# The low halves of the converted weights are subtracted on GpSimd in place of VectorE

## The chip, the cores and the metric

The kernel runs on one core of a Trainium2 chip. The metric is the device time of one execution, in microseconds (us). The kernel before was timed three times: 1189.03, 1189.84 and 1190.34 us, so the median is 1189.84 us. A core has five engines with instruction queues of their own: TensorE (PE, with the loading of its weights shown apart as PEld), VectorE (DVE), ScalarE (ACT), GpSimd (POOL) and SyncE (SP), which here issues all DMAs. Each queue is worked through in order; between queues there are semaphores.

## The reference

A linear attention is followed by a two-layer network. With batch 8, 8 heads, sequence 576 and head size 64:

```
proj = x @ w_phi;  proj -= max|proj| over the features
phi(x) = concat(exp(proj), exp(-proj))          # 2 x 128 features
kv = phi(k)^T v,   z = sum phi(k)
attn = (phi(q) kv) / (phi(q) z + 1e-6)
x = attn as 4608 tokens x 512
h = x @ w_in (512 x 2048);  g = max(0.01 h, h);  out = g @ w_out (2048 x 512)
```

The weights w_in and w_out arrive as 64-bit floating-point numbers, everything else as 32-bit ones. The result is in 32 bits.

## The kernel before

**Split products.** Most matrix products run in the type fp32r, which keeps fewer bits than fp32. To lose little, an operand a is split into a high half, a cast to fp32r, and a low half, a minus the high half, and a product becomes three: high by high, high by low and low by high. The high half is a cast (`copy_`, line 64), the low half a subtraction (`tt_`, line 71). Both helpers ask `pick` (line 59), which looks up an engine in the table `ENG` (line 35) by a key and goes round its letters: "v" is VectorE, "a" ScalarE, "p" GpSimd. A key that is not in the table gets ScalarE for a cast and GpSimd for a two-operand operation. So the low halves xl (of the attention's output), gl (of the first layer's result), ql and most of kpl (of the features) and vl run on GpSimd; the key "l", which belongs to the weights, says "v".

**The conversion of the weights.** `load_weights` (lines 161 to 187) takes w_in and w_out in 16 slices each, 32 steps in turn: w_in slice 0, w_out slice 0, w_in slice 1 and so on. A step loads 128 x 512 numbers of 64 bits (512 KB, line 172) into a staging place: halves of the ring in the first 10 steps, then parts of early buffers (f4, f1), then qs and the ring again. It builds the 32-bit numbers from the two words of each: the absolute value of the upper word (ScalarE, line 177) goes into w, a tile with the tag ql, clamped (VectorE, 178), shifted and masked (179) and joined with the two top bits (180); the lower word is scaled into cr, tag kvl (ScalarE, 182), and added (183, both as 32-bit whole numbers). Then come the high half (ScalarE, line 185, shown as line 67) and the low half (line 186, shown as line 72). The results stay in SBUF: the tiles w0h, w0l, w1h and w1l, each of 4 slices. The tag ql has two buffers, so step n+2 begins to write when the low half of step n has been read; kvl has one.

**The layers.** The tokens are worked through in 18 blocks of 256. `layer1` (line 592 on) is 12 matmuls of 128 x 256 for one slice: at each of four depths w0h and w0l with xh (lines 595 and 596), then four of w0h with xl (598). Leaky ReLU follows on ScalarE (602), then gh and gl. `layer2` adds to an accumulator in PSUM: w1h with gh (615), w1l with gh (616), w1h with gl (617). It runs three steps behind `layer1`. The first two blocks go through the 16 slices in alternation, so that each slice is used twice once it is converted; the others follow one by one with all slices in SBUF.

**The attention.** `k_phase` and `q_phase` work on pairs of heads. The first batch has its own functions (`first_k_phase`, `first_q_phase`), run before and beside the first conversion steps. In `first_q_phase` each pair goes through projection (425), maximum and subtraction (VectorE, 507 and 509), transposition on TensorE (515), exponentials (ScalarE, 522 and 523), product (537), copies to the ring and dn (ScalarE, 540 and 541), reciprocals of the denominators through two transpositions (VectorE, 544 to 547), and a multiplication into the ring on GpSimd. `split` makes xh (ScalarE) and xl (GpSimd) of it. In later batches, lines 216, 296 and 347 are low halves written out on VectorE. `load_k` and `load_q` load the next pair; after the v loads, a memset on GpSimd (198) fills two columns of the tile rv.

**The order.** It is not written out by hand. Each instruction has a priority, set by `tc.cur_priority`: the first batch comes ahead of the rest of the attention, that ahead of the conversion (`PW`), and this ahead of the layers. A scheduler simulates the engines and puts on each the ready instruction of the highest priority; the order of each queue is fixed then, and the chip follows it.

Of the kernel before, what the change touches and what calls it, by code (L numbers as in the profile page):

```python
# [31 lines left out]
NK = 8  # L32
BUFS = {"kk": 4, "pmk": 2, "eq": 2, "m4": 3, "m4n": 2, "g": 2, "gh": 2, "gl": 2, "qh": 2, "ql": 2, "dn": 2}
PBUFS = {"a": 3, "c": 1, "h": 2, "acc": 2}
ENG = {"vh": "a", "kst": "v", "qh": "v", "o": "av", "kpl": "pppv", "ksub": "vvp", "l": "v"}
TINY = 2.0 ** -15
HUGE = 2.0 ** 16 * 1.875
PF = -10 ** 6
# [6 lines left out]
def attention_moe_kernel(ctx: ExitStack, tc: tile.TileContext, q, k, v, vt, w_phi, w_in, w_out, out):  # L45
# [13 lines left out]
    def pick(key):  # L59
        n = cnt[key] = cnt.get(key, -1) + 1  # L60
        e = ENG.get(key, "")
        return e[n % len(e)] if e else None
# [648 lines left out]
```

## Time and profile before

One execution was recorded by the profiler. Its own time is 1187.94 us, and its span, from the first instruction to the last, is 1186.2 us.

| | before |
|---|---|
| median of three runs | 1189.84 us |
| the profiled execution, its time | 1187.94 us |
| its span | 1186.2 us |
| granted TensorE clock | 1.00 |
| GpSimd subtractions for gl, number and mean | 288, 827 ns |
| conversion steps, number | 32 |
| first and last start of line 177 | 20.0 and 175.8 us |
| last low half of the weights starts | 184.5 us |

To read it: a group of the profile names the line, the engine, the operation, output and inputs, the shape, how often it ran, the busy time in us and the mean time of one in ns; behind the second bar stands the engine's idle time ahead of these instructions, and what ended it. The line is often that of a helper (67, 69 and 72 are the casts and two-operand operations of `copy_` and `tt_`), so the output's name tells which it is. Slices are fortieths of the span, 29.7 us each, in tenths of busy time. A wait is given as "who <- for whom: us in total, times, longest". TensorE's matmuls overlap each other, so a TensorE that is always busy may still have gaps of less than one matmul.

### The profile page before, as it was taken

The page shows a single profiled execution, that of the slowest core. Times are in us where ns is not written, and L with a number is a line of the kernel's source. Part 1 is how long each engine was busy: PE and PEld are TensorE (multiplying, and loading weights), DVE is VectorE, ACT ScalarE, POOL GpSimd, SP SyncE. Part 2 cuts the span into 40 slices and gives each one's busy share as a digit, 9 for nine tenths or more (in the row PEclk, how much of TensorE's full clock was granted, in tenths as well). Part 3 has the DMA queues.
Part 4 walks back from the last instruction along what each step waited for, and adds up shares of the span by engine and source line. Part 5 has one row for each costly group of instructions (what it writes and reads, how often), then busy time and mean ns, then how long its engine had stood idle before and what let it go on. Part 6 is the DMA issues. An engine that isn't in the chain of part 4 may idle for free.

```text
span 1186.2 us, 21604 instructions
## 1 busy us (share of the span) xinstructions
PE 1153.7 (97%) x7496; PEld 1026.5 (87%) x7496; DVE 769.2 (65%) x1326; ACT 861.3 (73%) x2266; POOL 632.7 (53%) x709
## 2 busy tenths in 40 slices
PE   8899999899998999999999999999999999999998
PEld 5677778799887989889999999999999989899997
DVE  5988995587788778777777777757777765200000
ACT  5978775878788778777888878868887785433232
POOL 0131222576576667666666666757666666433232
PEclk9999999999999999999999999999999999999999
DMA  8436331211111111111111111101111100000000
GB/s 218 135 91 168 103 108 36 70 41 34 51 33 50 34 34 29 42 34 30 52 33 51 33 51 26 48 23 40 33 50 34 40 3 20 1 19 9 10 19 18
DMA packets 71005, 57.88 MB, mean 49 GB/s; under 512 B 53232, under 2 KB 54512, under 8 KB 70896
## 3 DMA queue, kind: packets, MB, share of 16 engines
q1 hardware_dynamic: 70896, 56.51, 17.1%
q8 instruction: 59, 0.97, 0.3%
q14 instruction: 50, 0.41, 0.1%
HBM read 46.27 MB, written 9.44 MB: 47 GB/s over the span
## 4 chain that ended last, share of the span: by engine, by line
PE 47%; DVE 2%; DMA 1%; issue 0%; ACT 0%; POOL 0%; SPq 0%; DVEq 0%; ACTq 0%; POOLq 0%
PE h L598 6%; PE h L596 6%; PE h L595 6%; PE acc L616 6%; PE acc L617 6%; PE acc L615 6%; PE c L228 3%; PE a L409 1%; PE a L404 1%; PE a L406 1%; PE a L251 1%; PE a L365 1%; PE a L364 1%; DVE tq L381 0%; DMA mx<-mx 0%
## 5 line engine op out<-in xcount | busy, mean ns | idle before, releaser
L72 POOL TENSOR_TENSOR gl<-g,gh 128x256 fp32r<-128x256 f32 x288 | 237.3, 827 | 305.4 <-ACT gh L67 220.2
L595 PE MATMUL h<-xh,w0h 128*128 128x256 f32 x1088 | 278.8, 283 | 2.4 <-ACT xh L67 1.3
L596 PE MATMUL h<-xh,w0l 128*128 128x256 f32 x1088 | 276.6, 281 | 0.0
L595 PEld LDWEIGHTS h<-xh,w0h 128*128 128x128 f32 x1088 | 205.4, 189 | 12.4 <-ACT g L602 2.4
L615 PE MATMUL acc<-w1h,gh 128*128 128x512 f32 x544 | 214.3, 394 | 0.2 <-DVE o L69 0.2
L616 PE MATMUL acc<-w1l,gh 128*128 128x512 f32 x544 | 213.3, 392 | 0.0
L596 PEld LDWEIGHTS h<-xh,w0l 128*128 128x128 f32 x1088 | 205.3, 189 | 8.4 <-issue 0.4
L617 PE MATMUL acc<-w1h,gl 128*128 128x512 f32 x544 | 203.5, 395 | 2.6 <-POOL rv L198 1.2
L598 PE MATMUL h<-xl,w0h 128*128 128x256 f32 x1088 | 191.2, 281 | 0.0
L602 ACT ACTIVATE g<-h 128x256 f32<-128x256 f32 x288 | 108.3, 381 | 106.0 <-PE h L598 83.0
L72 POOL TENSOR_TENSOR ql<-eq,qh 128x576 fp32r<-128x576 f32 x96 | 142.9, 1500 | 53.3 <-DVE qh L395 44.3
L67 ACT CAST gh<-g 128x256 fp32r<-128x256 f32 x288 | 115.2, 403 | 63.0 <-PE acc L616 60.9
L598 PEld LDWEIGHTS h<-xl,w0h 128*128 128x128 f32 x1088 | 155.9, 188 | 0.9 <-issue 0.4
L72 POOL TENSOR_TENSOR kpl<-ek,kph 128x512 fp32r<-128x512 f32 x72 | 101.5, 1410 | 75.9 <-ACT kph L67 59.3
L617 PEld LDWEIGHTS acc<-w1h,gl 128*128 128x128 f32 x544 | 99.5, 188 | 19.5 <-POOL rv L198 1.4
L69 DVE COPY o<-acc 128x512 f32<-128x512 f32 x17 | 11.7, 688 | 161.0 <-DMA out_dram<-o 118.0
L615 PEld LDWEIGHTS acc<-w1h,gh 128*128 128x128 f32 x544 | 102.5, 188 | 12.1 <-DVE o L69 0.4
L616 PEld LDWEIGHTS acc<-w1l,gh 128*128 128x128 f32 x544 | 102.3, 188 | 11.7
L282 ACT ACTIVATE ek<-pmk,m 128x128 f32<-128x128 f32 (+1 forms) x240 | 89.5, 390 | 13.5 <-DVE m L259 13.1
L281 ACT ACTIVATE ek<-pmk,m4n 128x128 f32<-128x128 f32 (+1 forms) x240 | 90.1, 392 | 8.6 <-DVE m4n L265 3.9
L395 DVE TENSOR_REDUCE qh<-eq 128x576 fp32r<-128x576 f32 x96 | 69.0, 751 | 25.7 <-ACT eq L389 22.9
L256 DVE TENSOR_TENSOR pmk<-a,pmk 128x256 f32<-128x256 f32 (+1 forms) x120 | 49.6, 420 | 54.0 <-ACT pmk L67 52.0
(183 smaller groups left out, 2404.8 us busy)
## 6 DMA issues: line engine op xcount, KB each, us to landing
out_dram<-o SPq DMA_DIRECT2D x36, 256.0 KB, 2.1
rq<-in_q_dram SPq DMA_DIRECT2D x28, 288.0 KB, 2.9
rk<-in_k_dram SPq DMA_DIRECT2D x27, 288.0 KB, 2.8
rv<-in_v_dram SPq DMA_DIRECT2D x29, 256.0 KB, 3.5
ring<-in_w_in_dram SPq DMA_DIRECT2D x9, 512.0 KB, 3.7
f<-in_w_out_dram SPq DMA_DIRECT2D x7, 512.0 KB, 3.6
f<-in_w_in_dram SPq DMA_DIRECT2D x7, 512.0 KB, 3.6
ring<-in_w_out_dram SPq DMA_DIRECT2D x5, 512.0 KB, 3.8
```

The costliest lines, as they stand in the source:

```text
L67: nc.scalar.copy(o, i)
L72: (nc.vector if pick(key) == "v" else nc.gpsimd).tensor_tensor(o, a, b, op=op)
L281: nc.scalar.activation(ek[r, j, 0:F], pmk[r, h], AF.Exp, bias=m4n[r, h : h + 1])
L282: nc.scalar.activation(ek[r, j, F:256], pmk[r, h], AF.Exp, scale=-1.0, bias=m4[r, h : h + 1])
L395: nc.vector.tensor_reduce(qh, eq.unsqueeze(3), axis=AX.X, op=ALU.max)
L595: nc.tensor.matmul(ph, lhsT=weight(0, "h", ft)[:, d * P : d * P + P], rhs=xh[d], start=d == 0, stop=False)
L596: nc.tensor.matmul(ph, lhsT=weight(0, "l", ft)[:, d * P : d * P + P], rhs=xh[d], start=False, stop=False)
L598: nc.tensor.matmul(ph, lhsT=weight(0, "h", ft)[:, d * P : d * P + P], rhs=xl[d], start=False, stop=d == NP - 1)
L602: nc.scalar.activation(g, ph, AF.Prelu, alpha=0.01)
L615: nc.tensor.matmul(a, lhsT=gh[:, ts], rhs=weight(1, "h", ft), start=ft == 0, stop=False)
L616: nc.tensor.matmul(a, lhsT=gh[:, ts], rhs=weight(1, "l", ft), start=False, stop=False)
L617: nc.tensor.matmul(a, lhsT=gl[:, ts], rhs=weight(1, "h", ft), start=False, stop=ft == NFT - 1)
```

## The change

In the table of engines the key "l" says "p". `tt_("l", ...)` in line 186 is its only use, so all 32 subtractions of the conversion are issued on GpSimd. Operation, shape and operands stay the same; the semaphores and the order of all queues are made anew by the scheduler.

```diff
-ENG = {"vh": "a", "kst": "v", "qh": "v", "o": "av", "kpl": "pppv", "ksub": "vvp", "l": "v"}
+ENG = {"vh": "a", "kst": "v", "qh": "v", "o": "av", "kpl": "pppv", "ksub": "vvp", "l": "p"}
```

## The prediction

> **What bounds the kernel now.** I read the page first: engine shares, the slices, the chain.
>
> ```profile
> span 1186.2 us, 21604 instructions
> PE 1153.7 (97%) x7496; PEld 1026.5 (87%) x7496; DVE 769.2 (65%) x1326; ACT 861.3 (73%) x2266; POOL 632.7 (53%) x709
> ...
> PE   8899999899998999999999999999999999999998
> DVE  5988995587788778777777777757777765200000
> ACT  5978775878788778777888878868887785433232
> POOL 0131222576576667666666666757666666433232
> ...
> PE 47%; DVE 2%; DMA 1%; issue 0%; ACT 0%; POOL 0%; SPq 0%; DVEq 0%; ACTq 0%; POOLq 0%
> ```
>
> TensorE is busy nearly everywhere, and nearly all of the chain that could be followed back is TensorE's (47% of the span against 2% for VectorE). So time is only won or lost where TensorE stands idle. VectorE is fullest in slices 1 to 5 (30 to 180 us), where the weights are converted, and GpSimd is nearly empty there. Next, the busy time by stage: the stage in which the first conversion steps share the engines with the first attention phases (20 to 70), a pause, the rest of the conversion (85 to 186), and what follows.
>
> ```profile
> core 0: us, PE busy (x) PEld busy (x) DVE busy (x) ACT busy (x) POOL busy (x), PEclk, DMA share, GB/s
> 20.00:70.00 50.00, 43.19 (x214) 30.83 (x213) 46.37 (x93) 46.44 (x103) 9.87 (x12) 1.00 0.47 138
> 70.00:85.00 15.00, 14.85 (x86) 12.14 (x87) 10.71 (x26) 9.24 (x25) 4.72 (x7) 1.00 0.38 121
> 85.00:186.00 101.00, 98.86 (x540) 76.60 (x538) 92.61 (x165) 78.67 (x184) 21.85 (x29) 1.00 0.42 117
> 186.00:240.00 54.00, 50.07 (x312) 42.45 (x311) 28.82 (x53) 38.81 (x107) 23.71 (x33) 1.00 0.18 52
> 240.00:800.00 560.00, 551.71 (x3772) 505.73 (x3772) 420.48 (x705) 456.92 (x1236) 374.32 (x386) 1.00 0.14 38
> 800.00:1186.00 386.00, 379.18 (x2518) 347.16 (x2516) 161.46 (x271) 223.85 (x603) 197.03 (x230) 1.00 0.08 23
> ```
>
> TensorE's idle time is 50 - 43.19 = 6.81 us in 20:70, 101 - 98.86 = 2.14 us in 85:186, 3.93 us in 186:240, and 8.29 + 6.82 = 15.1 us in everything after 240. The stage from 20 to 70 is the only one in which the conversion could cost TensorE much: VectorE and ScalarE are both full there, with 3.63 and 3.56 us idle in 50. In 85:186 VectorE has 8.4 us idle of 101, but TensorE hardly waits.
>
> Last, I asked how early the low halves are ready. Here is the first and the last low half of w_in (16 there are, and 16 of w_out), each with its own first matmul: line 596 runs four matmuls a step, so the first of its 1152 uses w_in's slice 0, and the 121st slice 15.
>
> ```profile
> 25.26 0.69 DVE L72 TENSOR_TENSOR w0l<-ql,w0h 128x512 fp32r<-128x512 f32 x1
> ...
> 58.63 0.28 PE L596 MATMUL h<-xh,w0l 128*128 128x256 f32 x1
> ...
> 180.28 1.22 DVE L72 TENSOR_TENSOR w0l<-ql,w0h 128x512 fp32r<-128x512 f32 x1
> ...
> 212.75 0.28 PE L596 MATMUL h<-xh,w0l 128*128 128x256 f32 x1
> ```
>
> The first is done at 25.95 and used at 58.63, the last at 181.50 and used at 212.75: 32.7 and 31.3 us of margin. Counting the same way through all 32, no margin is under 31 us. The conversion is work done in advance; nobody on TensorE waits for a low half.
>
> **The change, part by part.** What leaves VectorE and what GpSimd takes over:
>
> ```profile
> L72 DVE TENSOR_TENSOR w0l<-ql,w0h 128x512 fp32r<-128x512 f32 x16 | 12.3, 766 | 0.1
> L72 DVE TENSOR_TENSOR w1l<-ql,w1h 128x512 fp32r<-128x512 f32 x16 | 11.5, 716 | 0.4
> L183 DVE CUSTOM_DVE_ANT_0 ql<-ql,kvl 128x1024 uint16<-128x1024 uint16 x32 | 22.2, 694 | 0.6
> L72 POOL TENSOR_TENSOR kpl<-ek,kph 128x512 fp32r<-128x512 f32 x72 | 101.5, 1410 | 75.9 <-ACT kph L67 59.3 <-PE acc L616 5.7 <-PE c L228 3.5
> ```
>
> Removed from VectorE: 12.3 + 11.5 = 23.8 us in 32 instructions. Added to GpSimd: the trace has the same operation and shape there, kpl, at a mean of 1410 ns, so 32 x 1.41 = 45.1 us. Its busy time from 20 to 186 us rises from 36 (9.87 + 4.72 + 21.85) to about 81 of 166 us, so GpSimd does not become the bound. That kpl runs on GpSimd in this very form also says that the change will do what it says. No DMA moves.
>
> The margin first: a low half is done later by 1.41 - 0.74 = 0.67 us plus a wait in GpSimd's queue. Against 31 us of margin that costs nothing; the cover is the 31 us themselves, and it would take a queue 20 instructions deep to use it up. In 85:186 the price is therefore near zero from this side, and the 22 instructions that VectorE loses there (16 us) gain near zero too, since TensorE has only 2.14 us to win.
>
> What counts is 20:70. What leaves VectorE there:
>
> ```profile
> 20.00:70.00 50.00, 1.36 (x5) 0.94 (x5) 3.91 (x5) 1.00 0.47 138
> ...
> 20.00:70.00 50.00, 0.78 (x2) 0.38 (x2) 3.05 (x4) 1.00 0.47 138
> ```
>
> (the third pair of busy time and count is VectorE's; first w_in's low halves, then w_out's): 3.91 + 3.05 = 6.96 us, nine instructions. But VectorE does not get all of it, because the two engines get in each other's way:
>
> ```profile
> 92.32 0.73 POOL L72 TENSOR_TENSOR gl<-g,gh 128x256 fp32r<-128x256 f32 x1 [0.20 <-ACT gh L67]
> ...
> 92.44 1.15 DVE L183 CUSTOM_DVE_ANT_0 ql<-ql,kvl 128x1024 uint16<-128x1024 uint16 x1
> ...
> L72 DVE TENSOR_TENSOR kpl<-ek,kph x24: 644/792/1593, 233.2 to 984.8; 128x512 fp32r<-128x512 f32 x24
> L296 DVE TENSOR_TENSOR kst<-ek,kst x24: 686/1186/1808, 238.4 to 987.1; 64x512 fp32r<-64x512 f32 x24
> ```
>
> A conversion instruction of line 183 (694 ns in the mean) started 0.12 us into a GpSimd subtraction and took 1.15 us, ending 0.54 us after it. The last two rows are VectorE instructions that often meet the long GpSimd subtractions (minimum/median/maximum ns): they reach 1593 and 1808 from minima of 644 and 686, with medians 0.15 and 0.50 us above the minimum. So a GpSimd low half costs VectorE somewhere between nothing and its own 1.3 us; I take the 0.50 of line 296, whose neighbours in time are just such subtractions. For nine: 4.5 us. VectorE's net relief in 20:70 is 6.96 - 4.5 = 2.5 us.
>
> Who profits from it? The waits in that stage:
>
> ```profile
> PE c L537 <- ACT eq L522: 1.9, 1, 1.9
> PE h L595 <- ACT xh L67: 1.3, 2, 0.7
> PE h L537 <- ACT dn L541: 1.0, 1, 1.0
> ...
> ACT ql L177 <- DVE w1l L72: 0.5, 1, 0.5
> ...
> PE a L515 <- DVE pm L509: 0.4, 1, 0.4
> ```
>
> TensorE's larger waits end on ScalarE (1.9, 1.3, 1.0 us), only a 0.4 us one on VectorE. ScalarE itself has 3.56 us idle to give, and what is late next when VectorE is faster is ScalarE, whose work stays the same. I credit half of the relief: -1.25 us.
>
> The added wait. A low half now waits in GpSimd's queue for the cast of the high half on ScalarE, and behind it stand the products with the reciprocal denominators (ring), the low halves of x (xl) and of g (gl), and the memset of the next v tile (rv), on which SP's queue waits:
>
> ```profile
> ACT g L602 <- POOL gl L72: 19.4, 28, 2.3
> PE acc L617 <- POOL gl L72: 0.8, 2, 0.6
> SPq L195 <- POOL rv L198: 12.4, 5, 4.0
> ```
>
> Over the whole run ScalarE waited 19.4 us for gl and TensorE 0.8, so GpSimd's queue seldom reaches TensorE. SP's 12.4 us of waits delay loads that are issued a head ahead of their use; at nothing, and if that cover were gone, one subtraction, 1.4 us, a load. In 20:70 a product delayed by one subtraction delays xh on ScalarE, for which TensorE waits already (1.3 us above): I add 1.0 us, between 0 and 2 x 1.41.
>
> The turn of the two buffers of ql. Line 177 of step n+2 writes the buffer that the low half of step n has read, and it stands in ScalarE's queue ahead of the exponentials. A turn that is tight today gets 0.67 us longer. In 20:70 the one such wait is 0.5 us: +0.7 us, between 0 and 8 x 0.67 = 5.4 us were all eight turns tight.
>
> Sum: -1.25 + 1.0 + 0.7 = +0.45 us. The profiled execution took 1187.94 us, 1.74 us more than its span, and 1.90 us less than the median of the runs; so 1188.4 for it and 1190.3 as a median. From no change a measurement here can tell about 0.2%, 2.4 us, so this is within it.
>
> **The rivals.** *The planner deals another order.* The scheduler places every instruction by simulated times, so 32 changed costs can move instructions long after the conversion. What it can win there is bounded by TensorE's idle 15.1 us after 240; a quarter of it, 3.8 us, in either direction gives 1186.0 or 1193.6. Against it: nothing after 186 us is edited. I give it 0.22, more of it upward (0.14) since the chain shows little left to win.
>
> *Slower: the shared access to SBUF decides, in 20:70.* If every low half on GpSimd holds VectorE up for as long as it runs, nine cost 9 x 1.3 = 11.7 us and save 6.96: VectorE needs 4.7 us more in a stage where it has 3.63 us idle, little of it usable since most is waiting for ScalarE. TensorE then comes later by up to 4.7 us: 1195.0. It decides from a price of 6.96/9 = 0.77 us a low half upward. For it: the 1.15 us above, and the maxima of 1593 and 1808. Against it: the medians, 0.15 and 0.50 us, lie under the threshold. [...] Chance 0.22.
>
> *Faster: VectorE's relief passes through.* If VectorE is what holds up ScalarE in 20:70 (it feeds the exponentials and the denominators), TensorE can win up to ScalarE's idle 3.56 us there, and a part of the 2.14 us in 85:186, say half: -4.6 us, 1185.2. For it: VectorE is the fullest of the helpers over 85:186 (92%). Against it: the waits above. Chance 0.16.
>
> **How the numbers follow.** My forecast, no change that can be told, has 0.40; its own range is 1187.5 to 1192.2. Slower is 0.22 + 0.14 = 0.36, faster 0.16 + 0.08 = 0.24. The range takes in 1185.2 and 1195.0, and beyond them the uncertain ends: the ql turns and the products at their upper bounds (5.4 and 2.8 us instead of 0.7 and 1.0) reach 1196.8, and the planner adds to either; 1184.5 to 1198.0, with about one in ten left out on each side.
>
> **What would show it.** Right: 32 new GpSimd rows of w0l and w1l at 1.3 to 1.45 us; VectorE's busy time in 20:186 lower by some 8 to 16 us rather than 24, with lines 178 to 183 longer in the mean; first uses of the low halves still over 25 us after them; TensorE's idle time in 20:70 within 2 us of 6.81. Wrong: TensorE waiting for w0l or w1l; TensorE's idle time in 20:70 over 10 or under 4 us; or a difference in the idle time after 240, which would be the planner's doing.

## The result and the profile after

| | before | after |
|---|---|---|
| median (lowest to highest), four runs each | 1189.43 us (1188.57 to 1190.34) | 1196.23 us (1195.41 to 1196.75) |
| profiled execution, its time | 1187.94 us | 1195.41 us |
| its span | 1186.2 us | 1193.6 us |
| granted TensorE clock | 1.00 | 0.995 |

The time after is 1.0059 times that before, with a 95% interval of 1.0044 to 1.0074: slower by 0.6%, 6.8 us between the medians. The page after, with its slices for VectorE and GpSimd:

```profile
span 1193.6 us, 21587 instructions
PE 1157.9 (97%) x7496; PEld 1031.1 (86%) x7496; DVE 762.9 (64%) x1294; ACT 863.2 (72%) x2266; POOL 672.8 (56%) x741
...
DVE  5978996567678678777777777767777776200000
...
POOL 0354553556676676656766676766666666433232
```

The 32 instructions have moved: VectorE's count is 1294 after 1326, GpSimd's 741 after 709, and GpSimd is no longer empty in slices 1 to 6. GpSimd's busy time rose by 40.1 us. VectorE's fell by 6.3 us only, where 23.8 us of subtractions left it. Next, the stages after (PE, PEld, DVE, ACT, POOL, then the clock):

```profile
20.00:70.00 50.00, 42.72 (x208) 31.00 (x207) 45.35 (x83) 45.32 (x100) 20.27 (x19) 0.97 0.48 136
70.00:85.00 15.00, 14.75 (x82) 11.76 (x80) 10.07 (x23) 8.97 (x25) 7.00 (x9) 1.00 0.31 90
85.00:186.00 101.00, 93.60 (x493) 71.02 (x492) 93.11 (x141) 77.41 (x176) 48.59 (x46) 0.98 0.42 120
186.00:240.00 54.00, 51.40 (x309) 43.30 (x307) 28.46 (x50) 36.60 (x99) 24.62 (x35) 1.00 0.15 37
240.00:800.00 560.00, 552.72 (x3785) 508.30 (x3785) 413.94 (x711) 459.13 (x1241) 372.45 (x387) 1.00 0.15 40
```

TensorE's idle time, stage length minus busy time, is where the loss shows. In 20:70 it is 7.28 us, 0.47 more than before. In 85:186 it is 7.40 us against 2.14: 5.3 us more. In 186:240 it is 2.60 against 3.93, and in 240:800 7.28 against 8.29, so part is given back. VectorE did 165 instructions in 85:186 before and 141 now, yet was busy for 93.11 us against 92.61. The work that left was made up for by the rest becoming longer. Here are the conversion's own VectorE lines, after and then before, as groups of instructions:

```profile
L183 DVE CUSTOM_DVE_ANT_0 ql<-ql,kvl 128x1024 uint16<-128x1024 uint16 x32 | 27.6, 861 | 4.3 <-ACT kvl L182 2.4
L179 DVE TENSOR_SCALAR ql<-ql 128x512 int32<-128x512 int32 x32 | 21.0, 658 | 0.5
L178 DVE TENSOR_SCALAR ql<-ql 128x512 f32<-128x512 f32 x32 | 17.2, 541 | 4.3 <-ACT ql L177 4.1
L180 DVE SCALAR_TENSOR_TENSOR ql<-f,ql 128x512 int32<-128x512 int32 x14 | 14.3, 1025 | 0.3
L180 DVE SCALAR_TENSOR_TENSOR ql<-ring,ql 128x512 int32<-128x512 int32 x14 | 10.8, 771 | 0.3
L180 DVE SCALAR_TENSOR_TENSOR ql<-qs,ql 128x512 int32<-128x512 int32 x4 | 5.6, 1405 | 0.1
```

```profile
L179 DVE TENSOR_SCALAR ql<-ql 128x512 int32<-128x512 int32 x32 | 15.9, 497 | 0.4
L178 DVE TENSOR_SCALAR ql<-ql 128x512 f32<-128x512 f32 x32 | 14.5, 454 | 8.0 <-ACT ql L177 7.5
L180 DVE SCALAR_TENSOR_TENSOR ql<-f,ql 128x512 int32<-128x512 int32 x14 | 10.5, 752 | 0.2
L180 DVE SCALAR_TENSOR_TENSOR ql<-ring,ql 128x512 int32<-128x512 int32 x14 | 9.8, 699 | 0.1
L180 DVE SCALAR_TENSOR_TENSOR ql<-qs,ql 128x512 int32<-128x512 int32 x4 | 3.3, 823 | 0.0
```

The counts are the same. With the 22.2 us of line 183 before, these groups add up to 76.2 us before and 96.5 us after: 20.3 us more, or 20.3 / 32 = 0.63 us for each low half on GpSimd. Of 23.8 us taken off VectorE, 3.5 us are left. The next rows show how this happens. They are VectorE's and then GpSimd's instructions in time (start, duration), a few us before TensorE's longest gap:

```profile
122.77 0.88 DVE L179 TENSOR_SCALAR ql<-ql 128x512 int32<-128x512 int32 x1
123.68 1.64 DVE L180 SCALAR_TENSOR_TENSOR ql<-f,ql 128x512 int32<-128x512 int32 x1
125.46 0.99 DVE L183 CUSTOM_DVE_ANT_0 ql<-ql,kvl 128x1024 uint16<-128x1024 uint16 x1
...
127.55 1.20 DVE L178 TENSOR_SCALAR ql<-ql 128x512 f32<-128x512 f32 x1
128.79 0.43 DVE L179 TENSOR_SCALAR ql<-ql 128x512 int32<-128x512 int32 x1
129.25 0.69 DVE L180 SCALAR_TENSOR_TENSOR ql<-f,ql 128x512 int32<-128x512 int32 x1
...
130.46 0.68 DVE L183 CUSTOM_DVE_ANT_0 ql<-ql,kvl 128x1024 uint16<-128x1024 uint16 x1
131.06 0.42 DVE L178 TENSOR_SCALAR ql<-ql 128x512 f32<-128x512 f32 x1
131.40 0.68 DVE L262 TENSOR_TENSOR pmk<-a,m 128x512 f32<-128x512 f32 x1
```

```profile
123.32 1.46 POOL L72 TENSOR_TENSOR w0l<-ql,w0h 128x512 fp32r<-128x512 f32 x1
124.74 1.17 POOL L72 TENSOR_TENSOR gl<-g,gh 128x256 fp32r<-128x256 f32 x1
127.19 1.29 POOL L72 TENSOR_TENSOR w1l<-ql,w1h 128x512 fp32r<-128x512 f32 x1 [1.28 <-ACT w1h L67]
```

```profile
132.23 0.72 PE L362 MATMUL a<-rq,bd 64*128 64x288 f32 x2 [2.51 <-DVE pmk L262]
```

The subtraction from 123.32 to 124.78 lies on VectorE's line 180, which takes 1.64 us and ends at 125.32. The one from 127.19 to 128.48 lies on line 178, which takes 1.20 us and ends at 128.75, just after it. The subtraction for gl (124.74 to 125.91) lies on line 183, which takes 0.99 us. Line 179 takes 0.88 us at 122.77. A moment later, with no GpSimd subtraction beside them, the lines 179, 180, 183 and 178 take 0.43, 0.69, 0.68 and 0.42 us: the four instructions beside GpSimd were together 2.5 us longer. Behind these instructions in VectorE's queue stands line 262, which reads one of the three PSUM tiles with the tag a. It runs from 131.40 to 132.08, and TensorE, which needs that tile, starts at 132.23 after 2.51 us of idle time.

For the low halves themselves TensorE waits nowhere. They take on GpSimd nearly what the prediction said (minimum/median/maximum in ns):

```profile
L72 POOL TENSOR_TENSOR w0l<-ql,w0h x16: 1272/1292/1520, 23.9 to 186.9; 128x512 fp32r<-128x512 f32 x16
L72 POOL TENSOR_TENSOR w1l<-ql,w1h x16: 1274/1300/1737, 30.6 to 190.5; 128x512 fp32r<-128x512 f32 x16
```

From their ends to their first uses there are 34.7 to 64.7 us.

### The profile page after: what moved, and what is told of

Its sections match the earlier page's. It is cut to its first block, busy times and chain, and to the rows that moved or that the text cites. A ratio compares the mean times of both kernels' runs of the same rounds, so it can differ in the third digit from the quotient of the medians.

```text
span 1193.6 us, 21587 instructions
## 1 busy us (share of the span) xinstructions
PE 1157.9 (97%) x7496; PEld 1031.1 (86%) x7496; DVE 762.9 (64%) x1294; ACT 863.2 (72%) x2266; POOL 672.8 (56%) x741
## 4 chain that ended last, share of the span: by engine, by line
PE 72%; DVE 12%; ACT 6%; DMA 3%; issue 3%; POOL 2%; SPq 1%; DVEq 0%; POOLq 0%; ACTq 0%
PE h L598 9%; PE h L595 9%; PE h L596 9%; PE acc L617 9%; PE acc L616 8%; PE acc L615 8%; PE c L228 5%; PE a L404 2%; PE a L409 2%; PE a L251 2%; PE a L406 2%; DVE ql L180 2%; DVE tq L381 2%; DVE ql L183 1%; PE a L364 1%
## 5 line engine op out<-in xcount | busy, mean ns | idle before, releaser
L72 POOL TENSOR_TENSOR gl<-g,gh 128x256 fp32r<-128x256 f32 x288 | 234.8, 819 | 248.7 <-ACT gh L67 181.3
L595 PEld LDWEIGHTS h<-xh,w0h 128*128 128x128 f32 x1088 | 205.5, 189 | 10.9 <-ACT g L602 2.5
L395 DVE TENSOR_REDUCE qh<-eq 128x576 fp32r<-128x576 f32 x96 | 69.0, 751 | 25.6 <-ACT eq L389 19.9
```

Source lines behind the costliest of these rows:

```text
L72: (nc.vector if pick(key) == "v" else nc.gpsimd).tensor_tensor(o, a, b, op=op)
L395: nc.vector.tensor_reduce(qh, eq.unsqueeze(3), axis=AX.X, op=ALU.max)
L595: nc.tensor.matmul(ph, lhsT=weight(0, "h", ft)[:, d * P : d * P + P], rhs=xh[d], start=d == 0, stop=False)
```

## The experiments

The theory was that a GpSimd instruction that reads SBUF holds VectorE's instructions up, so VectorE stays as full as it was and is late where TensorE waits for it. The rivals were that the load on GpSimd or the later release of the two ql buffers costs the time, that the late low halves do, or that only the scheduler's new order does. Ratios are to the kernel before, run on the same chip beside them (medians 1188.88 us for e1 to e4, 1189.91 for e5 to e8, 1189.88 for e9 to e12). The edits of e1, e2 and e4 to e7 are made to the kernel before, those of the others to the changed kernel. Counts of differing TensorE instructions in the expectations partly include the numbers of buffers. Compared by the kernel's line at each place in the order, e1 differs from after in 116 of TensorE's 7496 matmuls, all of them among the first 1000, and from before in 1516. Nine of the twelve times fell outside the ranges that were expected, three of them (e3, e5, e7) by less than 0.4 us; those of e2, e9 and e11 fell inside. The part behind e12 shows why the times are so hard to foretell.

**e1, only the first ten steps on GpSimd.**

```diff
-ENG = {"vh": "a", "kst": "v", "qh": "v", "o": "av", "kpl": "pppv", "ksub": "vvp", "l": "v"}
+ENG = {"vh": "a", "kst": "v", "qh": "v", "o": "av", "kpl": "pppv", "ksub": "vvp", "l": "p" * 10 + "v" * 22}
```

> Low halves on GpSimd in the first 10 conversion steps alone (20 to 74 us), on VectorE in the other 22. Shared access to SBUF: lines 178 to 183 on VectorE lengthen in these ten steps only; TensorE's idle time in 85:186 goes back to about 2 us and at most one stretch at half clock is left, so 1190 to 1193 us. Order: TensorE's order here is far closer to that of the changed kernel (210 lines of difference) than to that of the kernel before (2392), so if the order is the cause the time stays at 1195 to 1197.

Measured: 1186.48 us, 0.9981 [0.9972, 0.9989].

```profile
85.00:190.00 105.00, 101.48 (x553) 78.30 (x552) 94.38 (x168) 81.44 (x189) 23.13 (x29) 1.00 0.43 121
```

**e2, only the last 22 on GpSimd.**

```diff
-ENG = {"vh": "a", "kst": "v", "qh": "v", "o": "av", "kpl": "pppv", "ksub": "vvp", "l": "v"}
+ENG = {"vh": "a", "kst": "v", "qh": "v", "o": "av", "kpl": "pppv", "ksub": "vvp", "l": "v" * 10 + "p" * 22}
```

> The counterpart: the last 22 low halves on GpSimd, the first 10 on VectorE. Shared access: collisions in 85:190 only, where TensorE's idle time grew by 5 us, so most of the loss stays: 1193 to 1196 us, with 20:70 as before. Order: TensorE's order is again closer to the changed kernel's (467 lines) than to that before (2284): 1195 to 1197.

Measured: 1193.15 us, 1.0037 [1.0024, 1.0051].

```profile
85.00:190.00 105.00, 95.63 (x488) 69.92 (x487) 95.24 (x145) 77.07 (x178) 51.45 (x48) 0.98 0.40 115
```

The two rows are the stage of the last 22 steps. With these on VectorE (e1) TensorE is idle for 3.52 us in it, with these on GpSimd (e2) for 9.37 us. So the loss arises there. From e1 to after, whose TensorE orders are nearly alike, only the engine of the last 22 steps changes, and the ratio goes from 0.9981 to 1.0059. (e2's profiled run took 1199.04 us at a clock of 0.989, against a median of 1193.15, so its span isn't compared.) The two halves do not add up: -0.19% and +0.37% against +0.59% together, so the order has a part in each number.

**e3, zeros in place of the low halves** (the low halves are left out; GpSimd only writes zeros).

```diff
-                tt_("l", l, w, h.bitcast(F32), ALU.subtract)
+                nc.gpsimd.memset(l.bitcast(F32), 0.0)
```

> The low halves are left out: GpSimd fills the tiles with zeros, so it writes as much but reads nothing, and VectorE is relieved of its 24 us. Shared access: lines 178 to 183 return to near 0.43, 0.43, 0.70 and 0.69 us in the mean, VectorE's work in the conversion falls from 96 to 76 us, and the time is 1184 to 1190 us. Order: TensorE's order stays close to that of the changed kernel (435 lines of difference against 2477), so 1194 to 1197 whatever VectorE does.

Measured: 1190.32 us, 1.0006 [0.9997, 1.0016]. VectorE's conversion lines take 79.2 us, close to the 76.2 before: most of the delay is gone. The time is no better than before, though. But this edit changes more than the reading. A memset waits for no ql, so 24 of the 32 run in the first 12.3 us of the span, ahead of the conversion, and the other eight in two groups from 146.34 and 153.77 us. VectorE's conversion has then hardly a memset beside it. The buffers of ql also come free earlier: the last high half ends at 177.6 us, where it ends at 190.4 after. So this run shows VectorE without the subtractions beside it, not beside a GpSimd that only writes; e12 tests that.

**e4, the load without the relief**: low halves on VectorE as before, and each subtracted on GpSimd once more into a spare tile.

```diff
                 tt_("l", l, w, h.bitcast(F32), ALU.subtract)
+                nc.gpsimd.tensor_tensor(st([P, DM], F32R, "o", "spare"), w, h.bitcast(F32), op=ALU.subtract)
```

> VectorE computes the low halves as before, and GpSimd computes all 32 once more into a tile that nobody reads (the tile of the outputs, free until the first output). Shared access: VectorE is slowed by the same collisions without being relieved, some 20 us more in the conversion lines than before the change (100 to about 120 us), TensorE's idle time in 20:190 grows by 5 to 12 us: 1196 to 1203. Relief matters little and order is the cause: the order is new here too, anywhere from 1188 to 1197, without the lines growing by 20 us being felt.

Measured: 1205.23 us, 1.0128 [1.0113, 1.0142]. VectorE's low halves themselves:

```profile
L72 DVE TENSOR_TENSOR w0l<-ql,w0h 128x512 fp32r<-128x512 f32 x16 | 19.0, 1186 | 0.0
L72 DVE TENSOR_TENSOR w1l<-ql,w1h 128x512 fp32r<-128x512 f32 x16 | 15.7, 983 | 0.1
```

They took 766 and 716 ns before. All of VectorE's conversion together went from 76.2 + 23.8 to 90.9 + 34.7 us: 25.6 us more for 32 GpSimd instructions, 0.80 us each. The load is dear by itself; the change is cheaper only because it also relieves.

**e5, order alone**: the two lines that make cr moved ahead of line 177, on the kernel before. No engine and no operand changes.

```diff
+                cr = st([P, DM], I32, "kvl")
+                nc.scalar.activation(cr, low.bitcast(U32), AF.Copy, scale=2.0 ** -29)
                 nc.scalar.activation(w, top.bitcast(F32), AF.Abs)
...
-                cr = st([P, DM], I32, "kvl")
-                nc.scalar.activation(cr, low.bitcast(U32), AF.Copy, scale=2.0 ** -29)
```

> The kernel before with one line moved: the lower word is scaled into cr ahead of the absolute value of the upper one. No engine changes, the planner only deals another order (304 lines of difference on TensorE). If an order by itself moves the time by microseconds, it shows here as 1186 to 1193, with VectorE's conversion lines as before (100 us); if the engine matters and not the order, 1188.5 to 1190.

Measured: 1193.13 us, 1.0028 [1.0019, 1.0037]. So another order of the same work is worth 3.2 us, nearly half of what the change costs. Every ratio here has to be read with that in mind.

**e6, only the first five on GpSimd.**

```diff
-ENG = {"vh": "a", "kst": "v", "qh": "v", "o": "av", "kpl": "pppv", "ksub": "vvp", "l": "v"}
+ENG = {"vh": "a", "kst": "v", "qh": "v", "o": "av", "kpl": "pppv", "ksub": "vvp", "l": "p" * 5 + "v" * 27}
```

> Low halves on GpSimd in the first five steps alone, in which GpSimd is idle otherwise. TensorE's order stays near that of the kernel before (584 lines of difference; 2363 to that of the first 10 on GpSimd). If relief of VectorE in 20:70 made the first 10 faster, half of it shows: 1187.5 to 1188.3. If the gain came from the other order (less TensorE idle time from 190 to 800 us), none of it shows: 1188.5 to 1190.5, and the idle time in 190:240 is near 3.9 us.

Measured: 1195.01 us, 1.0044 [1.0028, 1.0061]. Five subtractions cost more than ten (e1). More load cannot explain that; the order dealt along with it can: from the 1000th matmul on, e6 has another order than e1 and takes 8.0 us longer (table behind e12). For the first steps nothing can be said of the engine alone.

**e7, the last 22 as zeros on GpSimd**, the first ten on VectorE (these 22 low halves are left out).

```diff
-                tt_("l", l, w, h.bitcast(F32), ALU.subtract)
+                tt_("l", l, w, h.bitcast(F32), ALU.subtract) if n < 10 else nc.gpsimd.memset(l.bitcast(F32), 0.0)
```

> As the kernel with the last 22 low halves on GpSimd, but GpSimd fills these 22 with zeros and reads nothing; these low halves are left out. Shared access: lines 178 to 183 shorten again by 15 us and more, TensorE's idle time in 85:190 falls from 9.4 to below 5 us, and the time from 1193 to 1186 to 1190. If instead this order (521 lines from that of the changed kernel) is what costs, 1192 to 1194 as with the subtractions.

Measured: 1185.75 us, 0.9960 [0.9948, 0.9972], where the same 22 steps with reading subtractions (e2) gave 1.0037. VectorE's conversion lines: 77.7 us, against 92.3 in e2. As in e3, the buffers also come free earlier, and the memsets are not beside the conversion: 14 of the 22 run in the first 7.6 us.

**e8, each low half as four subtractions of 128 columns**, all on GpSimd: the same result and more load.

```diff
-                tt_("l", l, w, h.bitcast(F32), ALU.subtract)
+                [tt_("l", l[:, s : s + 128], w[:, s : s + 128], h[:, s : s + 128].bitcast(F32), ALU.subtract) for s in range(0, DM, 128)]
```

> The changed kernel with each low half in four subtractions of 128 columns, about 0.46 us each. If VectorE waits for the rest of one GpSimd instruction at a time, a collision costs at most 0.46 us instead of 1.3, but there are four times as many: VectorE's conversion lines at 90 to 105 us (96.5 in the changed kernel), no stall on TensorE of over 2 us between 20 and 190 us, fewer stretches at half clock, 1188 to 1194. If the order decides, anything: it differs in most lines from all others.

Measured: 1184.38 us, 0.9952 [0.9940, 0.9964]: faster than both kernels, in part by another order (table behind e12). GpSimd's pieces of w_in, and a VectorE line beside them:

```profile
L72 POOL TENSOR_TENSOR w0l<-ql,w0h 128x128 fp32r<-128x128 f32 x64 | 37.7, 619 | 16.9 <-ACT w0h L67 16.6
```

```profile
L180 DVE SCALAR_TENSOR_TENSOR ql<-f,ql 128x512 int32<-128x512 int32 x14 | 10.8, 781 | 0.3
```

With w_out's pieces GpSimd spends 73.3 us, 1.7 times the 43.8 of the change. But line 180 is back from 1025 to 781 ns, and the conversion lines take 81.9 us in all: 0.18 us for a low half instead of 0.63. What delays VectorE goes with the length of one GpSimd instruction, not with the sum.

**e9, the change in the order of e5; e10, the pieces in that order.** To the changed kernel and to e8 the same edit is made as in e5:

```diff
+                cr = st([P, DM], I32, "kvl")
+                nc.scalar.activation(cr, low.bitcast(U32), AF.Copy, scale=2.0 ** -29)
                 nc.scalar.activation(w, top.bitcast(F32), AF.Abs)
...
-                cr = st([P, DM], I32, "kvl")
-                nc.scalar.activation(cr, low.bitcast(U32), AF.Copy, scale=2.0 ** -29)
```

> The changed kernel with the same moved line as in the re-dealt kernel before. The engines are those of the change. If the engine is what costs, the time stays 3 us and more above the kernel before, 1193 to 1199, with the conversion lines of VectorE at 94 to 100 us; if the 6.8 us were the luck of one order, it can fall to 1189 to 1192.

> The low halves on GpSimd in four pieces, and the moved line. TensorE's order, tile numbers left aside, is close to the changed kernel's here (109 lines of difference; 631 to the kernel before). If short instructions on GpSimd are what makes the pieces fast, conversion lines at 80 to 86 us and 1183 to 1189; if the pieces had a lucky order, 1192 to 1197.

Measured: e9 1197.99 us, 1.0064 [1.0051, 1.0077]; e10 1191.21 us, 1.0010 [1.0002, 1.0019].

| low half on | order as dealt | with e5's moved lines |
|---|---|---|
| VectorE | 1 (before) | 1.0028 |
| GpSimd, whole | 1.0059 (after) | 1.0064 |
| GpSimd, in four | 0.9952 | 1.0010 |

VectorE's conversion lines take 78.2 us in e5, 97.5 in e9 and 83.5 in e10, so a low half costs 19.3 / 32 = 0.60 us whole and 0.17 us in four, nearly as in the order as dealt (0.63 and 0.18). That price of VectorE belongs to the engines. Down each column the signs of the times are the same too: whole low halves on GpSimd are slower than VectorE by 0.59% and by 1.0064 / 1.0028 = 0.36%; against VectorE, pieces are faster by 0.48% and by 0.18%. But a column isn't one order: the orders of its rows differ far behind the conversion. Only e9 and e10 share the whole order behind it, and there the pieces are faster than whole low halves by 1.0064 / 1.0010, which is 0.54%. The order moves the times by as much: the pieces alone differ by 0.58% between the columns.

**e11, two subtractions of 256 columns.**

```diff
-                tt_("l", l, w, h.bitcast(F32), ALU.subtract)
+                [tt_("l", l[:, s : s + 256], w[:, s : s + 256], h[:, s : s + 256].bitcast(F32), ALU.subtract) for s in range(0, DM, 256)]
```

> Two subtractions of 256 columns a low half, about 0.82 us each; TensorE's order nearly that of the changed kernel (67 lines, tile numbers left aside). If the price grows with the length of one GpSimd instruction, it lies between whole (96.5 us in the conversion lines, 1196) and quarters (82 us, 1184): 86 to 92 us and 1187 to 1193. If it is the sum of GpSimd's time that costs, it is above the whole ones: 100 us, 1196 and more.

Measured: 1191.62 us, 1.0008 [0.9996, 1.0020], between whole (1196.23) and quarters (1184.38), but no different from the quarters of e10 (1191.21), with which it shares the order from the 1000th matmul on.

```profile
L72 POOL TENSOR_TENSOR w0l<-ql,w0h 128x256 fp32r<-128x256 f32 x32 | 29.5, 944 | 22.5 <-ACT w0h L67 22.3
```

```profile
L180 DVE SCALAR_TENSOR_TENSOR ql<-f,ql 128x512 int32<-128x512 int32 x14 | 12.7, 912 | 0.3
```

Line 180 is between 1025 and 781 ns too, and VectorE's conversion lines take 90.0 us: 0.43 us a low half.

**e12, the load and the late release without the reading.** GpSimd subtracts only the first and the last eight columns, and fills the rest with two memsets between them (the other columns of the low halves are left out). It is then busy as long as in the change, and lets go of ql as late, but hardly reads.

```diff
-                tt_("l", l, w, h.bitcast(F32), ALU.subtract)
+                tt_("l", l[:, 0:8], w[:, 0:8], h[:, 0:8].bitcast(F32), ALU.subtract)
+                nc.gpsimd.memset(l[:, 0:508].bitcast(F32), 0.0)
+                nc.gpsimd.memset(l[:, 4:512].bitcast(F32), 0.0)
+                tt_("l", l[:, 504:512], w[:, 504:512], h[:, 504:512].bitcast(F32), ALU.subtract)
```

> GpSimd subtracts the first and the last 8 columns and in between fills the rest with zeros twice; the other low halves are left out. The buffer of ql is held as long as before and GpSimd is as busy (about 1.3 us a step), but it reads hardly anything. If reading is what holds VectorE up: conversion lines at 76 to 84 us and 1183 to 1190. If the later release of ql is what costs: lines as short, but 1193 to 1197, and the conversion ends at 190 us or later.

Measured: 1177.34 us, 0.9894 [0.9881, 0.9906].

```profile
L186 POOL MEMSET w0l<- 128x508 f32 x32 | 17.6, 550 | 1.6
...
L72 POOL TENSOR_TENSOR w0l<-ql,w0h 128x8 fp32r<-128x8 f32 x32 | 8.2, 258 | 21.4 <-ACT w0h L67 20.2
```

```profile
85.00:190.00 105.00, 100.84 (x552) 78.16 (x552) 84.66 (x150) 81.86 (x191) 56.16 (x115) 1.00 0.42 121
```

Four instructions a low half take 52.7 us with w_out's, more than the 43.8 of the change, and the conversion ends at 192.3 us, as in the change (191.8). VectorE is busy 84.66 us of this stage, and its conversion lines take 80.6 us in all, 4.4 us more than before. GpSimd's load, the release of ql and late low halves are all there, and the kernel is faster than before by 12.5 us. So none of the three explains a loss. What differs from the change is the reading and, with it, the order; the table below takes the two apart.

**The stage apart from the order behind it.** The traces of these runs say how much of each time arose where the edits act. In the table, the matmuls of TensorE are counted in the order in which they start. The first 1000 take in the conversion, and they are nearly the same 1000 in every run (at most 8 are others). From the 1000th on there are, but for e4, only three orders, the same at every place: that of after, that of before, and one that e8 and e12 share.

| last 22 low halves | run | 1000th matmul starts at, us | from there to the 6500th, us | order from the 1000th on |
|---|---|---|---|---|
| VectorE | before | 203.0 | 822.3 | before |
| VectorE | e5 | 205.6 | 822.2 | before |
| VectorE | e1 | 207.1 | 816.0 | after |
| VectorE | e6 | 208.3 | 824.0 | before |
| zeros, mostly early | e7 | 205.7 | 818.4 | after |
| zeros, mostly early | e3 | 209.6 | 816.8 | after |
| GpSimd, hardly reading | e12 | 205.5 | 809.3 | e8, e12 |
| GpSimd, in two | e11 | 211.2 | 815.6 | after |
| GpSimd, in four | e8 | 211.7 | 810.1 | e8, e12 |
| GpSimd, in four | e10 | 213.6 | 815.0 | after |
| GpSimd, whole | after | 214.8 | 818.0 | after |
| GpSimd, whole | e9 | 216.5 | 816.1 | after |
| GpSimd, whole | e2 | 218.1 | 818.2 | after |
| both engines | e4 | 221.9 | 821.8 | its own |

Each row is one profiled run, and stretches at half clock are part of it (by half of their length at most, which is 3.4 us of the first column in after, with two of them, and 8.5 in e2, with five). Even so the first column sorts the runs by what GpSimd reads beside VectorE. With all low halves on GpSimd it is 11.8 us longer than before, and 10.9 us longer from e5 to e9. The second column goes by the order, to within 3.4 us, and gives 4.3 us of that back. It also holds the whole gain of e12 over before: 13.0 us there, while its first 1000 matmuls take 2.5 us longer. So no run shows that TensorE gains from VectorE's relief, and most of the 6.8 us between e8 and e10 is the order. Of the 13 us by which e3 is slower than e12, the profiled runs have 4.1 in the first column and 7.5 in the second.

## Why the prediction was wrong, and where it was right

It said no change (1190.3 us); the kernel became slower, 1196.23, which lies inside the range of 1184.5 to 1198.0. That it lies there is partly luck: the conversion lost 11.8 us in the profiled runs, more than any rival had priced, and another order behind it gave 4.3 us back.

*The moved work: right.* 32 subtractions at medians of 1292 and 1300 ns stand on GpSimd, 43.8 us in all against 45.1 expected.

*The margins: right.* Over 31 us stayed over 31; TensorE waits for no low half.

*The step that failed* is the one for the stage from 85 to 186 us: "In 85:186 the price is therefore near zero from this side", and the gain near zero too. It looked at the low halves alone, and at what TensorE could win. What it can lose was left out: VectorE's delayed instructions also feed TensorE there, and TensorE's idle time went from 2.14 to 7.40 us. The delay of 0.50 us was charged to the nine low halves of 20:70 alone and put at nothing for the other 22. That is where e1 and e2 put the loss as well.

*What counts is 20:70: wrong.* Idle time there went from 6.81 to 7.28 us, as the sum (+0.45) had it, but the 22 steps behind it decided. The agreement doesn't confirm the terms. The turn of ql was put at +0.7 us; over the whole run, though, line 177 on ScalarE waited 2.1 us for the low halves after, against 7.1 before.

*The price of shared access: real, the size too small, the place wrong.* The prediction took 0.50 us a low half and had VectorE's busy time in 20:186 fall by 8 to 16 us. Measured are 0.63 us on the conversion's own lines, and 45.35 + 10.07 + 93.11 = 148.53 us against 149.69: 1.2 us less. The rival "slower" needed 0.77 us to decide, since it asked when VectorE would become fuller. It did not become fuller. VectorE came late at single moments, such as line 262 at 131.40, while its sum stayed. e4, e8, e11 and e12 together show it: the delay of VectorE's lines goes with the length of one reading GpSimd instruction (0.63, 0.43, 0.18 us for 512, 256 and 128 columns) and nearly goes away (4.4 us over 32 steps) when GpSimd mostly writes. The first 1000 matmuls go the same way only roughly: they end at 205.5 us where GpSimd hardly reads and at 214.8 with whole low halves, but halves and quarters don't differ (211.2, 211.7 and 213.6). The two-input lines 180 and 183 together grew by 12.5 us in the change and by 1.6 us in e12. The one-input lines 178 and 179 grew too, by 7.8 us in the change and 2.8 us in e12. By what means a reading GpSimd instruction holds these lines up is not shown.

*The planner's order: real, and larger than bounded.* The prediction allowed 3.8 us either way; e5 moved the time by 3.2 us with no other change. From the 1000th matmul on, the order of after is 4.3 us shorter than that of before, and that of e8 and e12 by 12 to 13 us.

*What was not in the sum: the clock.* TensorE's busy time rose by 4.2 us with the same 7496 matmuls. Here are stretches of the trace after, each of 3.41 us; the columns are as above, the first is TensorE's busy time and the third from the end the clock:

```profile
38.05:41.46 3.41, 1.56 (x10) 1.42 (x11) 3.41 (x7) 2.68 (x6) 1.31 (x1) 1.00 0.56 162
41.46:44.87 3.41, 3.41 (x17) 3.04 (x16) 3.38 (x7) 2.91 (x8) 0.00 (x0) 0.50 0.76 233
...
130.21:133.62 3.41, 1.39 (x6) 0.99 (x7) 3.38 (x7) 2.44 (x7) 1.27 (x1) 1.00 0.55 159
133.62:137.03 3.41, 3.41 (x15) 2.87 (x14) 3.35 (x6) 2.55 (x6) 1.47 (x2) 0.50 0.75 197
369.14:372.55 3.41, 1.58 (x10) 0.92 (x8) 3.10 (x4) 2.88 (x8) 1.14 (x1) 1.00 0.11 43
372.55:375.96 3.41, 3.22 (x16) 3.19 (x16) 1.62 (x5) 2.35 (x6) 3.15 (x3) 0.50 0.09 34
```

Three times a stretch in which TensorE is busy for under half is followed by one at a clock of 0.50. The profiled run of before has none until its end. So the two waits of 2.5 us, that of 132.23 and one of 2.47 us for VectorE's line 509 that ended at 39.90, are paid twice, and so is the series of shorter ones before 372.55: behind them matmuls take longer (the eight of line 515 from 41.46 us on took 421 ns each, where the median of all 36 is 273; the two of line 404 from 372.55 on took 442 and 578, where the median of 192 is 295). The busy time alone doesn't say what that costs, since it differs between kernels without such stretches too (1150.1 us in e12, 1153.7 before). The runs of before tell more: of the 74 beside the experiments, ten have a mean clock of at most 0.996 and take 1191.2 us in the mean, against a mean of 1189.7 for all. The runs after stand at 0.994 to 0.996. So the lower clock is worth about 1.5 of the 6.8 us by this comparison. It is an estimate; if TensorE had needed all of the clock that is missing, 0.995 against a mean of 0.998 for the 74, it would be about 3.3 us. Some 3.5 to 5 us remain.

*What stays open.* How the loss in the first 1000 matmuls divides exactly between VectorE's delays, the clock and the order, which differs there too (in 665 places between before and after, in 116 between e1 and after, in 417 between after and e12). Why e8 needs 6.2 us more than e12 for them, when VectorE's conversion lines are nearly the same in both (81.9 and 80.6 us). And what makes the order of e8 and e12 so much shorter behind the conversion: that order came with the edits of these two runs and was not tested apart from them.

## What to carry to other kernels

Before moving work from VectorE to GpSimd, ask what a reading GpSimd instruction does to VectorE's instructions beside it: here each long one gave back 0.63 of the 0.74 us that it had saved. If it has to go there, cut it into short instructions; with four of 128 columns VectorE lost 0.18 us instead of 0.63 though GpSimd worked 1.7 times as long, and under one order behind the conversion the kernel was 0.54% faster. And where a scheduler deals the order, first time the stage that the edit acts on apart from the rest: here another order of later work moved the whole by 4 to 13 us.

## What the hardware showed

The half-clock stretches lie on a fixed grid. In the trace after they begin at 41.46, 133.62 and 372.55 us and last 3.41 us each; the differences, 92.16 and 238.93 us, are 27 and 70 times 3.413 us. In e2 the later onsets (55.57 and 185.27 us) lie 5 and 43 such lengths behind the first, in e9 and e10 (141.60 and 141.20 us) 30. Laid on that grid, every stretch between 20 and 949 us of after, e2, e3, e5, e6, e7, e9 and e10 in which TensorE was busy for less than half was followed by half clock (seven, with 1.39 to 1.67 us busy), while those between a half and three quarters went either way (113.14 to 116.55 us after, with 1.86 us busy, was not followed by one; 35.79 to 39.20 us in e9, with 1.88 us, was). In after, single gaps of 2.51 and 2.47 us were enough.

Splitting a GpSimd instruction was expected to leave VectorE's conversion lines at 90 us or more. A 512-column low half took 1.29 us in one piece (the median of w_in's) and 4 x 0.60 us in four (the mean), and the lines fell from 96.5 to 81.9 us. The kernel was 11.8 us faster with it as dealt, and 6.8 us faster from e9 to e10, where the order behind the conversion is the same.
